# One PSUM pool and a reordered first stage in a linear-attention and gated-MLP block

## Chip, cores and metric

The kernel runs on one core of a Trainium2 chip. The metric is the device time of one execution in microseconds (us), of which some 2 us lie outside the span that the profile shows: 2.5 us in the profiled execution before. Medians are of several executions. A ratio is the mean time of one kernel's fast runs over that of the other's fast runs of the same rounds, so it is not quite the ratio of the medians that stand beside it.

Engines: PE is TensorE (matmuls), PEld its weight loads, DVE is VectorE, ACT is ScalarE, SP issues most of the DMAs. Timeline lines join neighbouring instructions of one kind; where a group reaches over the edge of the stretch that was asked for, only its part inside is counted.

## Reference

```python
# B=1, S=2048, D=1024, H=32 heads of 32, F=3584, all bf16
def A(x):                                   # linear attention
    q, k, v = split_heads(x @ wqkv)
    pq, pk = phi(q), phi(k)                 # where(t>0, t+1, exp(t)) + 1e-6
    kv = sum_s pk[s]^T v[s];  z = sum_s pk[s]
    return merge_heads((pq @ kv) / (pq @ z + 1e-6)) @ wo
def B(x):                                   # gated MLP
    return (relu(x @ W_gate) * (x @ W_up)) @ W_down
h  = x + A(layernorm(x))
h2 = h + B(layernorm(h))
```

## The kernel before

S is cut into 16 x tiles of 128 rows and 4 blocks of 512. The framework's scheduler puts each engine's instructions into one fixed order from their priorities and its own model; on the chip each engine then takes them in that order, each waiting for its semaphores. A tile drawn from a pool with `bufs=n` waits until the tile n draws earlier has been released.

```python
ps_a  = PSUM pool: tag "tp" 2 banks, tag "mm" 3 banks          # first stage
ps_kv = PSUM pool: kv_ps, 3 banks
for t in range(ST):                                            # 16 x tiles
    ... bn_stats, bn_aggr, Ln, Exp -> rstd;  xn = (x - mean) * rstd
    pt = ps_tp()
    for kc in range(KC):
        nc.tensor.transpose(pt[:, kc, :], xn[:, kc*P:(kc+1)*P], ident[:])
    nc.scalar.copy(out=xnT[:, :, t*P:(t+1)*P], in_=pt[:])      # 1.02 us
    for j in range(2 * NKB):                                   # 2 halves of K, 2 of V
        ps = ps_mm("kvp")
        for kc in range(KC):
            nc.tensor.matmul(ps, lhsT=xnT[:, kc, tile t], rhs=wkv_sb[:, kc, half j], ...)
        if j < NKB: phi_from_psum(ps, pk[half j])              # ACT exp, then two DVE operations
        else:       nc.scalar.copy(out=v_sb[half], in_=ps)
    for c in range(KC):
        nc.tensor.matmul(kv_ps[...], lhsT=pk[:, c], rhs=v_sb[:, c, :], ...)   # kv and z
    if t == 3: q_proj(0, ps_mm)
kvbd, zbd = kv_ps * mask;  q_proj(1, ps_mm)                    # pools ps_a, ps_kv end here

ps_b = PSUM pool: tags "tp", "pa", "pg", "pd", 2 banks each
attn_block(0)              # den, num, transposes, attn, LayerNorm, transposes of 4 tiles
q_proj(2), q_proj(3)       # on tag "pg": 2 banks; the scheduler mixes them into attn_block(0)
for b in range(4):
    attn_block(b + 1)      # mixed into the MLP by the scheduler
    mlp_block(b)           # gate on "pg", up on "pd", down on both
```

`q_proj(b)` makes pqT of block b: for each of 8 chunks, 8 matmuls into one bank, then phi into pqT. `attn_block(b)` starts with 32 tiny matmuls, `den<-zbd,pqT`.

## Time and profile before

| | before |
|---|---|
| time, median of 13 executions | 880.38 us (879.35 to 880.98) |
| span of the profiled execution | 878.0 us |
| matmuls | 5376 |

Summary of the profile page of the kernel before: the span, busy time by engine (share of the span, instructions), and the shares of the chain of work that ended last.

```profile
span 878.0 us, 12434 instructions
PE 854.8 (97%) x5376; PEld 488.7 (56%) x5376; DVE 288.9 (33%) x536; ACT 166.7 (19%) x305; POOL 3.6 (0%) x31
...
PE 94%; DVE 2%; ACT 2%; DMA 1%; issue 0%; SPq 0%; DVEq 0%
```

PE bounds the kernel.

The waits of PE in the kernel before: what PE waited for, us in total, number of times, longest.

```profile
PE tp L165 <- DVE xn L161: 9.0, 2, 6.0
PE kvp L173 <- ACT xnT L166: 4.6, 7, 0.7
PE qp L102 <- DVE pqT L88: 3.1, 3, 1.0
PE den L235 <- DVE pqT L88: 1.9, 1, 1.9
```

The head in the kernel before, from the timeline (start us, us, engine, line, operation, tiles, count, idle time before and what ended it): PE's first instructions, then two of ACT.

```profile
5.97 1.04 PE L165 MATMUL tp<-ident,xn 128*128 128x128 bf16 x8 [5.97 <-DVE xn L161]
10.06 0.93 PE L165 MATMUL tp<-ident,xn 128*128 128x128 bf16 x7 [3.06 <-DVE xn L161]
10.78 4.40 PE L173 MATMUL kvp<-wkv_sb,xnT 128*128 128x512 bf16 x11
...
9.22 0.20 ACT L159 ACTIVATE rstd<-lnv 128x1 f32<-128x1 f32 x1
9.33 0.99 ACT L166 COPY xnT<-tp 128x1024 bf16<-128x1024 bf16 x1
```

PE transposes tile 0 at 6 us, then stands for 3 us at the transposes of tile 1, which the order puts ahead of tile 0's first matmul. ACT copies tile 0 at 9.33 us only, behind tile 1's statistics.

The end of that stage in the kernel before (PE, then DVE), and one gap of the first attention block:

```profile
171.63 1.89 PE L102 MATMUL qp<-xnT,wq_sb 128*128 128x512 bf16 x8
175.40 0.96 PE L235 MATMUL den<-zbd,pqT 128*128 128x4 bf16 x32 [1.88 <-DVE pqT L88]
...
174.65 0.69 DVE L88 SCALAR_TENSOR_TENSOR pqT<-qp,phi_e 128x512 bf16<-128x512 f32 x1
...
187.76 0.59 PE L102 MATMUL qp<-xnT,wq_sb 128*128 128x512 bf16 x2 [1.03 <-DVE pqT L88]
```

### The profile page before, as it was taken

To read this page: it belongs to the slowest core of one execution; us is meant where nothing else is said; L and a number is where in the kernel's file an instruction comes from. 1 tells how busy PE (TensorE), PEld (TensorE's weight loads), DVE (VectorE), ACT (ScalarE), POOL (GpSimd) and SP (SyncE) were. 2 spreads that over 40 slices of the span, in tenths; PEclk is the share of its full clock that TensorE was granted. 3 is DMA by queue.
4 is the path that set the end of the run, shared out by engine and by line. 5 is a ranking of instruction groups with operands and counts; after the bars stand their busy time and mean duration, and the time that the engine had idled before them with its cause. 6 is when DMAs were issued, how large, how long until landed. Compare 5 with 4: busy or idle time off the path is not lost.

```text
span 878.0 us, 12434 instructions
## 1 busy us (share of the span) xinstructions
PE 854.8 (97%) x5376; PEld 488.7 (56%) x5376; DVE 288.9 (33%) x536; ACT 166.7 (19%) x305; POOL 3.6 (0%) x31
## 2 busy tenths in 40 slices
PE   5999999999999999999999999999999999999998
PEld 2444544444444445885444478744444885444687
DVE  4674332676762121116512110363212012212111
ACT  3443443322222111001211100022111001111100
POOL 0000000000000000000000000000000000000000
PEclk9999999999999999999999999999999999999999
DMA  9600000630024445651344555414353764353152
GB/s 322 228 25 25 1 1 1 216 96 25 13 76 153 149 140 184 189 167 61 120 154 135 191 175 174 133 49 133 130 190 111 217 180 136 127 192 97 42 174 73
DMA packets 133926, 109.85 MB, mean 125 GB/s; under 512 B 3824, under 2 KB 128752, under 8 KB 133872
## 3 DMA queue, kind: packets, MB, share of 16 engines
q1 hardware_dynamic: 133872, 109.07, 39.9%
q8 instruction: 42, 0.69, 0.3%
q14 instruction: 12, 0.10, 0.0%
HBM read 104.86 MB, written 4.19 MB: 124 GB/s over the span
## 4 chain that ended last, share of the span: by engine, by line
PE 94%; DVE 2%; ACT 2%; DMA 1%; issue 0%; SPq 0%; DVEq 0%
PE down L322 22%; PE gate L301 22%; PE up L305 21%; PE kvp L173 13%; PE attn L270 6%; PE qp L102 6%; PE tp L286 1%; PE kv_ps L184 1%; PE tp L260 1%; ACT xnT L166 1%; PE num L249 1%; DMA x_sb<-in_A_x_dram 1%; ACT v_sb L180 0%; DVE o_sb L253 0%; DVE h L272 0%; PE den L235 0%
## 5 line engine op out<-in xcount | busy, mean ns | idle before, releaser
L301 PE MATMUL gate<-hnT,wg_sb 128*128 128x512 bf16 x896 | 214.9, 379 | 0.0
L305 PE MATMUL up<-hnT,wu_sb 128*128 128x512 bf16 x896 | 214.6, 379 | 0.0
L322 PE MATMUL down<-wd_sb,hhT 128*128 128x256 bf16 x1792 | 196.3, 273 | 0.0
L322 PEld LDWEIGHTS <-hhT 128*128 128x128 bf16 x1792 | 175.3, 98 | 21.2
L309 DVE TENSOR_TENSOR hhT<-up,rg 128x512 bf16<-128x512 f32 x112 | 77.3, 690 | 269.4 <-PE up L305 266.6
L308 ACT ACTIVATE rg<-gate 128x512 bf16<-128x512 f32 x112 | 66.9, 597 | 474.2 <-PE gate L301 474.2
L305 PEld LDWEIGHTS <-wu_sb 128*128 128x128 bf16 x896 | 87.3, 98 | 102.4
L301 PEld LDWEIGHTS <-wg_sb 128*128 128x128 bf16 x896 | 86.8, 98 | 99.7
L173 PE MATMUL kvp<-wkv_sb,xnT 128*128 128x512 bf16 x512 | 116.4, 383 | 4.6 <-ACT xnT L166 4.6
L173 PEld LDWEIGHTS <-xnT 128*128 128x128 bf16 x512 | 49.3, 99 | 61.9 <-ACT xnT L166 5.8
L327 DVE TENSOR_TENSOR o_t<-down,h 128x256 bf16<-128x256 f32 x64 | 24.2, 419 | 171.4 <-PE down L322 169.5
L102 PE MATMUL qp<-xnT,wq_sb 128*128 128x512 bf16 x256 | 59.7, 379 | 3.1 <-DVE pqT L88 3.1
L270 PE MATMUL attn<-wo_sb,oT 128*128 128x512 bf16 x256 | 58.2, 380 | 0.0
L86 DVE TENSOR_SCALAR phi_e<-phi_e 128x512 f32<-128x512 f32 x64 | 26.9, 420 | 70.1 <-ACT phi_e L84 70.1
L270 PEld LDWEIGHTS <-oT 128*128 128x128 bf16 x256 | 23.8, 98 | 33.0 <-DVE oT L262 6.3
L102 PEld LDWEIGHTS <-wq_sb 128*128 128x128 bf16 x256 | 24.2, 98 | 29.0 <-issue 4.3
L272 DVE TENSOR_TENSOR h<-attn,x_res 128x512 bf16<-128x512 f32 x32 | 22.1, 691 | 32.8 <-PE attn L270 32.7
L84 ACT ACTIVATE phi_e<-qp 128x512 f32<-128x512 f32 x32 | 19.1, 597 | 50.4 <-PE qp L102 50.4
L84 ACT ACTIVATE phi_e<-kvp 128x512 f32<-128x512 f32 x32 | 19.1, 596 | 38.2 <-PE kvp L173 38.2
L180 ACT CAST v_sb<-kvp 128x512 bf16<-128x512 f32 x32 | 18.7, 585 | 32.9 <-PE kvp L173 32.9
L153 DVE BATCH_NORM_STATS2 stats<-x_sb 128x6 f32<-128x512 bf16 x32 | 20.6, 672 | 7.9 <-DMA x_sb<-in_A_x_dram 7.9
L88 DVE SCALAR_TENSOR_TENSOR pqT<-qp,phi_e 128x512 bf16<-128x512 f32 x32 | 22.1, 691 | 1.0
(41 smaller groups left out, 264.2 us busy)
## 6 DMA issues: line engine op xcount, KB each, us to landing
wg_sb<-in_B_W_gate_dram SPq DMA_DIRECT2D x28, 1024.0 KB, 5.2
wu_sb<-in_B_W_up_dram SPq DMA_DIRECT2D x28, 1024.0 KB, 7.4
wd_sb<-in_B_W_down_dram SPq DMA_DIRECT2D x112, 256.0 KB, 2.9
x_sb<-in_A_x_dram SPq DMA_DIRECT2D x16, 256.0 KB, 6.6
wkv_sb<-in_A_wqkv_dram SPq DMA_DIRECT2D x4, 1024.0 KB, 9.4
x_res<-in_A_x_dram SPq DMA_DIRECT2D x16, 256.0 KB, 2.6
out_dram<-o_t SPq DMA_DIRECT2D x32, 128.0 KB, 1.8
wq_sb<-in_A_wqkv_dram SPq DMA_DIRECT2D x2, 1024.0 KB, 11.2
```

Source lines behind the costliest of these rows:

```text
L84: nc.scalar.activation(out=e[:], in_=ps_ap, func=ACT.Exp)
L86: nc.vector.tensor_scalar(out=e2[:], in0=e[:], scalar1=1.0, scalar2=PHI_EPS, op0=ALU.min, op1=ALU.add)
L88: nc.vector.scalar_tensor_tensor(out=dst_ap, in0=ps_ap, scalar=0.0, in1=e2[:], op0=ALU.max, op1=ALU.add)
L102: nc.tensor.matmul(ps[:, :TB], lhsT=wq_sb[:, kc, c * P:(c + 1) * P], rhs=xnT[:, kc, b * TB:(b + 1) * TB], start=(kc == 0), stop=(kc == KC ...
L173: nc.tensor.matmul(ps[:, :NW], lhsT=xnT[:, kc, t * P:(t + 1) * P], rhs=wkv_sb[:, kc, j * NW:(j + 1) * NW], start=(kc == 0), stop=(kc == KC ...
L270: nc.tensor.matmul(ps[:, :NW], lhsT=oT[:, c, :], rhs=wo_sb[:, c, j * NW:(j + 1) * NW], start=(c == 0), stop=(c == KC - 1))
L301: nc.tensor.matmul(g_ps[:, :TB], lhsT=wg_sb[:, kc, fi * P:(fi + 1) * P], rhs=hnT[:, kc, :], start=(kc == 0), stop=(kc == KC - 1))
L305: nc.tensor.matmul(u_ps[:, :TB], lhsT=wu_sb[:, kc, fi * P:(fi + 1) * P], rhs=hnT[:, kc, :], start=(kc == 0), stop=(kc == KC - 1))
L308: nc.scalar.activation(out=rg[:], in_=g_ps[:, :TB], func=ACT.Relu)
L309: nc.vector.tensor_tensor(out=hhT[:, f, :], in0=u_ps[:, :TB], in1=rg[:], op=ALU.mult)
L322: nc.tensor.matmul(accs[tt // 2][:, tt % 2, :], lhsT=hhT[:, f, tt * P:(tt + 1) * P], rhs=wd_sb[:, fi, :], start=(f == 0 and tt % 2 == 0), ...
L327: nc.vector.tensor_tensor(out=o_ts[tt][:, q * QW:(q + 1) * QW], in0=accs[tt // 2][:, tt % 2, :], in1=h_tiles[t][:, q * QW:(q + 1) * QW], o ...
```

## The change

The intent is to keep PE from waiting in the first stage and at its borders:

- One PSUM pool for the whole kernel: tp 2 banks, x 2, y 4. kv_ps takes 3 of the y banks until the masks have read it. The late q_proj, gate, up and down share y.
- LayerNorm and transposes of tile t+1 come before K of tile t; K of four tiles comes before V of four tiles; the kv_ps matmuls come one tile late.
- The start is in a hand-made order on PE, ACT and DVE, and the first copy is split between DVE and ACT.
- Another DMA order at the start; half of the last stores are issued by ACT.

No matmul is added or removed. The core of the diff (cuts marked):

```diff
+    pspool = ctx.enter_context(tc.tile_pool(name="ps", bufs=1, space=PSUM))
+    def ps_x(nm="x"):  return pspool.tile([P, 512], FP32, tag="x", bufs=2, name=nm)
+    def ps_y(nm="y"):  return pspool.tile([P, 512], FP32, tag="y", bufs=4, name=nm)
+    def ps_xy(nm="xy"): ...                       # x, x, y in turn
-        ps_a = ...tile_pool(name="ps_a", ...)     # and ps_kv; ps_b after the first stage
-            return ps_a.tile([P, 512], FP32, tag="mm", bufs=3, name=nm)
+        ps_mm = ps_xy
+        kv_ps = [ps_y("kv_ps") for _ in range(n_kv_banks)]
...                                                # x0, wk0, x1, wk1, x2, x3, wv0, wv1, x4, ...
+            if t == 0 and KC >= 2:
+                nc.vector.tensor_copy(out=xnT[:, 0:KC // 2, tile t], in_=pt[:, 0:KC // 2, :])
+                nc.scalar.copy(out=xnT[:, KC // 2:KC, tile t], in_=pt[:, KC // 2:KC, :])
+            else:
+                nc.scalar.copy(out=xnT[:, :, t * P:(t + 1) * P], in_=pt[:])
...
+        with tc.manual_schedule(engines={ET.PE, ET.Activation, ET.DVE}):
+            ln_T(0)
+            xn1 = ln_x(1)
+            pk0 = kproj(0, [0])
+            tp_x(1, xn1)
+            kproj(0, [1], pk0)
+        for g in range(NTB):
+            for tt in range(TPB):                  # K of four tiles
+                ...
+                if t + 1 < ST: ln_T(t + 1)
+                pks[t] = kproj(t)
+                if tt == 0: kv_acc()
+            for tt in range(TPB):                  # V of four; kv_ps of the tile before
+                vproj_kv(t, pks.pop(t))
+            if g < NQA - 1: q_proj(g, ps_mm, kv_acc)
...
-                g_ps = ps_b.tile([P, 512], FP32, tag="pg", bufs=2, name="gate")
+                g_ps = ps_y("gate")
-        q_proj(b, lambda nm: ps_b.tile([P, 512], FP32, tag="pg", bufs=2, name=nm))
+        q_proj(b, ps_y)
...
+                    eng = nc.scalar if (last block, last quarter, tt % 2 == 1) else nc.sync
```

More of the change, by code (lines that the diff above doesn't have):

```diff
@@ L73, in block_kernel, with ps_tp, ps_x, ps_y @@
         nc.gpsimd.memset(mask[hh * Dh:(hh + 1) * Dh, P + hh:P + hh + 1], 1.0)
+    pspool = ctx.enter_context(tc.tile_pool(name="ps", bufs=1, space=PSUM))
+    _xy = [0]
+    def ps_tp():
+        return pspool.tile([P, KC, P], BF16, tag="tp", bufs=2, name="tp")
+    def ps_x(nm="x"):
+        return pspool.tile([P, 512], FP32, tag="x", bufs=2, name=nm)
+    def ps_y(nm="y"):
+        return pspool.tile([P, 512], FP32, tag="y", bufs=4, name=nm)
+    def ps_xy(nm="xy"):
+        _xy[0] += 1
+        return ps_x(nm) if _xy[0] % 3 != 0 else ps_y(nm)
     pq_pool = ctx.enter_context(tc.tile_pool(name="pq", bufs=1))
@@ L96, in block_kernel, with q_proj @@
     wqkv_v = wqkv.rearrange("(kc p) n -> p kc n", p=P)
-    def q_proj(b, ps_fn):
+    def q_proj(b, ps_fn, after_first=None):
         for c in range(KC):
@@ L105, in q_proj @@
             phi_from_psum(ps[:, :TB], pqT[:, c, b * TB:(b + 1) * TB], qwork, TB)
+            if c == 0 and after_first is not None:
+                after_first()
     NQA = min(2, NTB)
     with ExitStack() as actx:
-        ps_a = actx.enter_context(tc.tile_pool(name="ps_a", bufs=1, space=PSUM))
-        ps_kv = actx.enter_context(tc.tile_pool(name="ps_kv", bufs=1, space=PSUM))
         apool = actx.enter_context(tc.tile_pool(name="apool", bufs=1))
@@ L115, in block_kernel @@
         asmall = actx.enter_context(tc.tile_pool(name="asmall", bufs=4))
-        def ps_tp():
-            return ps_a.tile([P, KC, P], BF16, tag="tp", bufs=2, name="tp")
-        def ps_mm(nm="mm"):
-            return ps_a.tile([P, 512], FP32, tag="mm", bufs=3, name=nm)
+        ps_mm = ps_xy
         wkv_sb = apool.tile([P, KC, 2 * D], BF16, name="wkv_sb")
-        kv_ps = ps_kv.tile([P, n_kv_banks, 512], FP32, name="kv_ps")
+        kv_ps = [ps_y("kv_ps") for _ in range(n_kv_banks)]
         x_tiles = {}
@@ L133, in block_kernel @@
         load_x(0)
-        for j in range(2 * NKB):
+        nxt = 1
+        for j in range(NKB):
             nc.sync.dma_start(out=wkv_sb[:, :, j * NW:(j + 1) * NW],
                               in_=wqkv_v[:, :, D + j * NW:D + (j + 1) * NW])
-            if j == 0 and ST > 1:
-                load_x(1)
-        for t in range(2, min(4, ST)):
-            load_x(t)
+            if nxt < min(TPB, ST):
+                load_x(nxt)
+                nxt += 1
+        while nxt < min(TPB, ST):
+            load_x(nxt)
+            nxt += 1
+        for j in range(NKB, 2 * NKB):
+            nc.sync.dma_start(out=wkv_sb[:, :, j * NW:(j + 1) * NW],
+                              in_=wqkv_v[:, :, D + j * NW:D + (j + 1) * NW])
+        while nxt < min(6, ST):
+            load_x(nxt)
+            nxt += 1
         for j in range(NKB):
@@ L143, in block_kernel, with ln_x @@
         nc.sync.dma_start(out=wo_sb[:], in_=wo.rearrange("(kc p) n -> p kc n", p=P))
-        for t in range(ST):
+        def ln_x(t):
             if t not in x_tiles:
@@ L162, in block_kernel, with tp_x @@
                                     op0=ALU.subtract, op1=ALU.mult)
+            return xn
+        def tp_x(t, xn):
             pt = ps_tp()
@@ L165, in block_kernel, with ln_T, kproj @@
                 nc.tensor.transpose(pt[:, kc, :], xn[:, kc * P:(kc + 1) * P], ident[:])
-            nc.scalar.copy(out=xnT[:, :, t * P:(t + 1) * P], in_=pt[:])
-            pk = awork.tile([P, D], BF16, tag="pk", name="pk")
-            v_sb = awork.tile([P, KC, NDW], BF16, tag="v_sb", name="v_sb")
-            nc.gpsimd.memset(v_sb[:, :, P:NDW], 1.0)
-            for j in range(2 * NKB):
-                ps = ps_mm("kvp")
+            if t == 0 and KC >= 2:
+                nc.vector.tensor_copy(out=xnT[:, 0:KC // 2, t * P:(t + 1) * P], in_=pt[:, 0:KC // 2, :])
+                nc.scalar.copy(out=xnT[:, KC // 2:KC, t * P:(t + 1) * P], in_=pt[:, KC // 2:KC, :])
+            else:
+                nc.scalar.copy(out=xnT[:, :, t * P:(t + 1) * P], in_=pt[:])
+        def ln_T(t):
+            tp_x(t, ln_x(t))
+        def kproj(t, js=range(NKB), pk=None):
+            if pk is None:
+                pk = awork.tile([P, D], BF16, tag="pk", bufs=TPB + 2, name="pk")
+            for j in js:
+                ps = ps_mm("kp")
                 for kc in range(KC):
@@ L175, in block_kernel, with kv_acc @@
                                      start=(kc == 0), stop=(kc == KC - 1))
-                if j < NKB:
-                    phi_from_psum(ps[:, :NW], pk[:, j * NW:(j + 1) * NW], awork, NW)
-                else:
-                    jj = j - NKB
-                    nc.scalar.copy(out=v_sb[:, jj * CPB:(jj + 1) * CPB, 0:P],
-                                   in_=ps[:, :NW].rearrange("p (c e) -> p c e", e=P))
+                phi_from_psum(ps[:, :NW], pk[:, j * NW:(j + 1) * NW], awork, NW)
+            return pk
+        pend = []
+        def kv_acc():
+            if not pend:
+                return
+            t, pk, v_sb = pend.pop()
             for c in range(KC):
                 bnk, i = divmod(c, GPB)
-                nc.tensor.matmul(kv_ps[:, bnk, i * NDW:(i + 1) * NDW],
+                nc.tensor.matmul(kv_ps[bnk][:, i * NDW:(i + 1) * NDW],
                                  lhsT=pk[:, c * P:(c + 1) * P], rhs=v_sb[:, c, :],
@@ L187, in block_kernel @@
                                  skip_group_check=True)
-            if (t + 1) % TPB == 0 and t // TPB < NQA - 1:
-                q_proj(t // TPB, ps_mm)
-        for c in range(KC):
-            bnk, i = divmod(c, GPB)
-            nc.vector.tensor_tensor(out=kvbd[:, c, :], in0=kv_ps[:, bnk, i * NDW:i * NDW + P],
-                                    in1=mask[:, 0:P], op=ALU.mult)
-            nc.vector.tensor_tensor(out=zbd[:, c, :], in0=kv_ps[:, bnk, i * NDW + P:(i + 1) * NDW],
-                                    in1=mask[:, P:NDW], op=ALU.mult)
@@ L196, in block_kernel, with vproj_kv @@
-        q_proj(NQA - 1, ps_mm)
-    ps_b = ctx.enter_context(tc.tile_pool(name="ps_b", bufs=1, space=PSUM))
-    def ps_tp2():
-        return ps_b.tile([P, KC, P], BF16, tag="tp", bufs=2, name="tp")
-    def ps_pa(nm="pa"):
-        return ps_b.tile([P, 512], FP32, tag="pa", bufs=2, name=nm)
-    def ps_pg(nm="pg"):
-        return ps_b.tile([P, 2, HB], FP32, tag="pg", bufs=2, name=nm)
-    def ps_pd(nm="pd"):
-        return ps_b.tile([P, 2, QW], FP32, tag="pd", bufs=2, name=nm)
+        def vproj_kv(t, pk):
+            v_sb = awork.tile([P, KC, NDW], BF16, tag="v_sb", bufs=3, name="v_sb")
+            nc.gpsimd.memset(v_sb[:, :, P:NDW], 1.0)
+            for jj in range(NKB):
+                j = NKB + jj
+                ps = ps_mm("vp")
+                for kc in range(KC):
+                    nc.tensor.matmul(ps[:, :NW], lhsT=xnT[:, kc, t * P:(t + 1) * P],
+                                     rhs=wkv_sb[:, kc, j * NW:(j + 1) * NW],
+                                     start=(kc == 0), stop=(kc == KC - 1))
+                nc.scalar.copy(out=v_sb[:, jj * CPB:(jj + 1) * CPB, 0:P],
+                               in_=ps[:, :NW].rearrange("p (c e) -> p c e", e=P))
+            kv_acc()
+            pend.append((t, pk, v_sb))
@@ new lines, in block_kernel @@
+        ET = mybir.EngineType
+        with tc.manual_schedule(engines={ET.PE, ET.Activation, ET.DVE}):
[5 more added lines that the diff above has]
+        for g in range(NTB):
+            pks = {}
+            for tt in range(TPB):
+                t = g * TPB + tt
+                if t == 0:
+                    pks[0] = pk0
+                    continue
+                if t + 1 < ST:
+                    ln_T(t + 1)
+                pks[t] = kproj(t)
+                if tt == 0:
+                    kv_acc()
+            for tt in range(TPB):
+                t = g * TPB + tt
+                vproj_kv(t, pks.pop(t))
+            if g < NQA - 1:
+                q_proj(g, ps_mm, kv_acc)
@@ new lines, in last_kv @@
+        def last_kv():
+            kv_acc()
+            for c in range(KC):
+                bnk, i = divmod(c, GPB)
+                nc.vector.tensor_tensor(out=kvbd[:, c, :], in0=kv_ps[bnk][:, i * NDW:i * NDW + P],
+                                        in1=mask[:, 0:P], op=ALU.mult)
+                nc.vector.tensor_tensor(out=zbd[:, c, :], in0=kv_ps[bnk][:, i * NDW + P:(i + 1) * NDW],
+                                        in1=mask[:, P:NDW], op=ALU.mult)
+        q_proj(NQA - 1, ps_mm, last_kv)
@@ L212, in block_kernel, with ps_pair @@
+    ps_tp2 = ps_tp
+    ps_pa = ps_x
+    def ps_pair(nm="pair"):
+        return pspool.tile([P, 2, QW], FP32, tag="y", bufs=4, name=nm)
     bwork = ctx.enter_context(tc.tile_pool(name="bwork", bufs=2, side="right"))
@@ L302, in mlp_block @@
                                      start=(kc == 0), stop=(kc == KC - 1))
-                u_ps = ps_b.tile([P, 512], FP32, tag="pd", bufs=2, name="up")
+                u_ps = ps_y("up")
                 for kc in range(KC):
@@ L314, in mlp_block @@
         for q in range(NQ):
-            accs = [(ps_pg("down") if i % 2 == 0 else ps_pd("down")) for i in range(npair)]
+            accs = [ps_pair("down") for i in range(npair)]
             for g in range(NFG):
@@ L330, in mlp_block @@
                     q0 = q - (q % 2)
-                    nc.sync.dma_start(out=of[t * P:(t + 1) * P, q0 * QW:(q + 1) * QW],
-                                      in_=o_ts[tt][:, q0 * QW:(q + 1) * QW])
+                    eng = nc.scalar if (b == NTB - 1 and q == NQ - 1 and tt % 2 == 1) else nc.sync
+                    eng.dma_start(out=of[t * P:(t + 1) * P, q0 * QW:(q + 1) * QW],
+                                  in_=o_ts[tt][:, q0 * QW:(q + 1) * QW])
         for tt in range(TPB):
```

## The prediction

> **What bounds it now.** TensorE: the page has PE busy 854.8 of 878.0 us and PE 94% of the chain that ended last. Eight 128x512 matmuls take 1.73 us (216 ns each; timeline), 448 down matmuls 48.91 us (109 ns each); from 270 to 395 us PE has no idle. No matmul is added or removed, so only idle or slow PE time can be won. By timeline, chain and waits that is:
>
> - Head: the first K/V matmul starts at 10.78 us. PE's order puts 7 transposes of x tile 1 (landed 7.42, xn done 10.0) ahead of it, and the ACT copy of tile 0's transpose, ready at 7.0, stands behind tile 1's statistics (9.33).
> - The first 8 matmuls run 427 ns apart, until about 14.4 us. The Trainium skill (TensorE: Matmul & The Clock Gate, the HAM clock gate) says the array runs at half clock until about 3.4 us of activity; the trace agrees, although the clock view shows 1.00. About 1.7 us, which stays.
> - Attention-input stage, to 173.5 us: 16.85 us per two x tiles. At pure rate 64 matmuls of 216 ns and 32 small ones of 56 to 58 ns take 15.7: 1.1 us lost, nearly all PE waiting for ACT's 1.02 us xnT copy. About 7 pairs: 8 us.
> - Then 1.9 us before den and three waits of 1.03 us in the first attention block, all for DVE writing pqT (q_proj has two PSUM buffers there).
> - Tail: last matmuls near 874.3, four output DMAs issued in 1.82 us, end at 878.
>
> **What the change does.** One PSUM pool (tp 2, x 2, y 4 banks); K of four tiles, then V of four; transposes of tile t+1 before K of tile t; kv_ps one tile late; a hand-ordered start with the first copy split on DVE and ACT; another DMA order; half of the last stores issued by ACT. The built order agrees: tp x8, kp x8, tp x8, kp x12.
>
> **Estimate (from the durations above).**
> 1. Head: K can start near 7.7 us (7.0 plus half a copy). But DVE's order has a statistic of x tile 2 before xn of tile 1, and that tile lands near 11 us (2.9 MB at some 330 GB/s): PE idles about 1.5 us there, and about 1.5 us for xn of tiles 2 and 4, as DVE carries phi (1.12 us per half) and statistics. Net gain 0.5.
> 2. xnT copy hidden behind 16 K matmuls, kv matmuls without waits: 7.
> 3. q_proj with four buffers: of 3.1 us, 2.5, as DVE comes near 90% there. The den wait stays: 0.2.
> 4. Tail: the skill (Trainium Kernel Development and Optimization, Key Constraints) says that issuing from several queues saves only issue time: 0.2.
> 5. MLP: same four banks, no idle: 0.
>
> Sum about 10.5: **869.5 us** predicted, 865.5 to 873.5 for 8 in 10. Faster by over 2% (under 862.4): 0.04; within 2%: 0.955; slower: 0.005.
>
> **Right if**: first K matmul near 7.7 us; PE idles 1 to 2 us before tile 1's transposes, xn behind a DMA wait; PE's wait for xnT (4.6 us) is gone; stage A ends near 166 us; the 1.03 us waits shrink to near nothing; MLP blocks keep their 167.0 us period.
>
> **Wrong if**: x tile 2 lands elsewhere; K phases become DVE-bound (phi 2.24 plus LayerNorm 2.06 us per tile against 3.94 of PE) and PSUM runs out; DVE delays the attention chain; shared y banks stall the MLP.

## More of the kernel before

The Trainium skill (Perfetto Trace Analysis, Identifying the Most-Contended Engine) warns that matmul busy time is a poor measure of the distance to the roofline because matmuls are pipelined, and this trace agrees: a 128x512 matmul is recorded as 379 ns long, but back to back they start 216 ns apart. So I count from start to start. At the spacing each shape reaches when nothing holds it (216 ns for 512 columns, 109 for 256, 57.5 for 132, 55.8 for 128, 25.5 for the 4 columns of den) the 5376 matmuls take 842.8 us, not 854.8. The remaining 35.2 us of the span are what any change of order can work on.

The steady state of the first stage in the kernel before, PE in the timeline:

```profile
75.50 0.40 PE L184 MATMUL kv_ps<-v_sb,pk 128*128 128x132 bf16 x4
75.73 0.66 PE L165 MATMUL tp<-ident,xn 128*128 128x128 bf16 x9
77.05 7.08 PE L173 MATMUL kvp<-wkv_sb,xnT 128*128 128x512 bf16 x32 [0.66 <-ACT xnT L166]
83.97 0.40 PE L184 MATMUL kv_ps<-v_sb,pk 128*128 128x132 bf16 x4
84.20 0.59 PE L173 MATMUL kvp<-wkv_sb,xnT 128*128 128x512 bf16 x2
84.81 0.39 PE L184 MATMUL kv_ps<-v_sb,pk 128*128 128x132 bf16 x4
```

There are two losses here. Before the 32 kvp matmuls PE waits for ACT's copy of the transposes. And the second four kv_ps matmuls start at 84.81 us, although the two kvp matmuls ahead of them need only 0.43 us from 84.20: another 0.17 us, with no idle time shown, because the kvp matmul's record covers it. They wait for ACT's copy of the second half of v_sb (in an earlier tile that copy ends at 27.93 us and these matmuls start at 27.98).

## The result

| | before | after |
|---|---|---|
| time, median | 880.38 us (13 executions) | 864.30 us (8 executions, 864.16 to 864.71) |
| ratio | | 0.9819 (0.9809 to 0.9828) |
| span of the profiled execution | 878.0 us | 862.1 us |

The change wins 16.1 us, 1.8%. The prediction was 10.5 us (869.5 us, range 865.5 to 873.5): within 2%, as forecast, but 1.2 us below the range.

The summary of the profile page after:

```profile
span 862.1 us, 12429 instructions
PE 850.3 (99%) x5376; PEld 487.8 (57%) x5376; DVE 288.5 (33%) x537; ACT 167.1 (19%) x305; POOL 3.3 (0%) x31
...
PE 95%; DVE 2%; DMA 1%; ACT 1%; issue 0%; SPq 0%; DVEq 0%
```

PE's waits after:

```profile
PE tp L188 <- DVE xn L181: 7.0, 2, 6.2
PE kp L204 <- DVE xnT L190: 0.5, 1, 0.5
PE tp L353 <- DVE hn L349: 0.2, 1, 0.2
```

Three of the four waits are gone. 6.2 of the 7.0 us left are the start itself. The head after, PE in the timeline, then DVE:

```profile
6.23 1.04 PE L188 MATMUL tp<-ident,xn 128*128 128x128 bf16 x8 [6.23 <-DVE xn L181]
7.79 3.59 PE L204 MATMUL kp<-wkv_sb,xnT 128*128 128x512 bf16 x8 [0.52 <-DVE xnT L190]
12.15 0.62 PE L188 MATMUL tp<-ident,xn 128*128 128x128 bf16 x8 [0.78 <-DVE xn L181]
12.61 2.75 PE L204 MATMUL kp<-wkv_sb,xnT 128*128 128x512 bf16 x12
...
10.96 0.69 DVE L173 BATCH_NORM_STATS2 stats<-x_sb 128x6 f32<-128x512 bf16 x1 [1.79 <-DMA x_sb<-in_A_x_dram]
11.57 0.53 DVE L181 TENSOR_SCALAR xn<-x_sb,mv,rstd 128x1024 bf16<-128x1024 bf16 x1
```

As predicted, K starts at 7.8 us, and xn of tile 1 stands in DVE's order behind a statistic of tile 2, which lands at 10.96 us.

The steady state after: no gap anywhere in these lines, and the 8 kv_ps matmuls of a tile run in one piece.

```profile
87.31 3.62 PE L204 MATMUL kp<-wkv_sb,xnT 128*128 128x512 bf16 x16
90.76 0.63 PE L218 MATMUL kv_ps<-v_sb,pk 128*128 128x132 bf16 x8
91.23 0.61 PE L188 MATMUL tp<-ident,xn 128*128 128x128 bf16 x8
91.67 3.62 PE L204 MATMUL kp<-wkv_sb,xnT 128*128 128x512 bf16 x16
```

The end of the stage and the first attention block after (PE, then DVE, then PE again):

```profile
159.81 3.83 PE L118 MATMUL qp<-xnT,wq_sb 128*128 128x512 bf16 x17
163.57 0.94 PE L302 MATMUL den<-zbd,pqT 128*128 128x4 bf16 x32
...
164.76 0.68 DVE L104 SCALAR_TENSOR_TENSOR pqT<-qp,phi_e 128x512 bf16<-128x512 f32 x1
...
174.20 3.40 PE L118 MATMUL qp<-xnT,wq_sb 128*128 128x512 bf16 x15
177.44 0.61 PE L353 MATMUL tp<-ident,hn 128*128 128x128 bf16 x8
```

den starts at 163.57 us, before DVE has even begun the last phi of q_proj(1) (164.76 us). So den never needed that data: den of block 0 reads what q_proj(0) wrote long before. My prediction had taken it for a data wait.

The whole difference, counted from start to start in the two traces (each row is the time by which matmuls start later than the pure rate allows, put to the wait named there; first and last row are the time before the first and after the last matmul):

| us | before | after | won | predicted |
|---|---|---|---|---|
| until the first transpose | 5.97 | 6.23 | | |
| waits in the head (first copy, xn of tiles 1, 2, 4) | 3.31 | 2.46 | | |
| half-rate matmuls at the start | 2.47 | 1.76 | | |
| these three, the head | 11.75 | 10.45 | 1.3 | 0.5 |
| K/V matmuls waiting for ACT's xnT copy | 5.79 | 0 | 5.8 | |
| kv_ps waiting for ACT's second v_sb copy | 2.97 | 0 | 3.0 | |
| these two | 8.76 | 0 | 8.8 | 7 |
| q_proj in the first attention block | 3.60 | 0 | 3.6 | 2.5 |
| den | 2.04 | 0.09 | 1.95 | 0.2 |
| all other | 5.2 | 5.1 | 0.1 | 0 |
| after the last matmul | 3.85 | 3.66 | 0.2 | 0.2 |
| sum | 35.2 | 19.3 | 15.9 | 10.4 |

### The profile page after: what moved, and what is told of

Its sections match the earlier page's. It is cut to its first block, busy times and chain, and to the rows that moved or that the text cites. A ratio compares the mean times of both kernels' runs of the same rounds, so it can differ in the third digit from the quotient of the medians.

```text
span 862.1 us, 12429 instructions
## 1 busy us (share of the span) xinstructions
PE 850.3 (99%) x5376; PEld 487.8 (57%) x5376; DVE 288.5 (33%) x537; ACT 167.1 (19%) x305; POOL 3.3 (0%) x31
## 4 chain that ended last, share of the span: by engine, by line
PE 95%; DVE 2%; DMA 1%; ACT 1%; issue 0%; SPq 0%; DVEq 0%
PE down L389 23%; PE gate L368 22%; PE up L372 22%; PE attn L337 7%; PE vp L230 6%; PE qp L118 6%; PE kp L204 5%; PE tp L353 1%; DMA x_sb<-in_A_x_dram 1%; PE num L316 1%; PE kv_ps L218 1%; PE tp L327 1%; PE tp L188 1%; DVE stats L173 0%; PE den L302 0%; DVE hn L349 0%
## 5 line engine op out<-in xcount | busy, mean ns | idle before, releaser
L204 PE MATMUL kp<-wkv_sb,xnT 128*128 128x512 bf16 x256 | 59.6, 387 | 0.5 <-DVE xnT L190 0.5
L230 PE MATMUL vp<-wkv_sb,xnT 128*128 128x512 bf16 x256 | 57.2, 379 | 0.0
L233 ACT CAST v_sb<-vp 128x512 bf16<-128x512 f32 x32 | 18.7, 584 | 35.1 <-PE vp L230 35.1
```

The source lines that it names most:

```text
L204: nc.tensor.matmul(ps[:, :NW], lhsT=xnT[:, kc, t * P:(t + 1) * P], rhs=wkv_sb[:, kc, j * NW:(j + 1) * NW], start=(kc == 0), stop=(kc == KC ...
L230: nc.tensor.matmul(ps[:, :NW], lhsT=xnT[:, kc, t * P:(t + 1) * P], rhs=wkv_sb[:, kc, j * NW:(j + 1) * NW], start=(kc == 0), stop=(kc == KC ...
```

## Experiments

All twelve runs gave correct results. "The control" is the changed kernel itself, run again.

### One pool, the bank counts left alone (b_onepool)

Is the wait before den the handover from one set of PSUM pools to the next? This is the kernel before with its three pools made into one. Each use keeps as many banks as it had; only the borders between pools go.

```diff
-        ps_a  = ...tile_pool(name="ps_a", bufs=1, space=PSUM)
-        ps_kv = ...tile_pool(name="ps_kv", bufs=1, space=PSUM)
-            return ps_a.tile([P, 512], FP32, tag="mm", bufs=3, name=nm)
+            tag = "pa" if _n[0] % 3 != 0 else "pg"
+            return ps_b.tile([P, 512], FP32, tag=tag, bufs=2, name=nm)
-        kv_ps = ps_kv.tile([P, n_kv_banks, 512], FP32, name="kv_ps")
+        kv_ps = [ps_b.tile([P, 512], FP32, tag=tg, bufs=2, name="kv_ps") for tg in ("pg", "pd", "pd")]
```

> The kernel before, with one PSUM pool for the whole kernel in place of three (the bank counts stay: tp 2, matmul 3 and kv 3 in the first stage, q_proj 2 later). Theory A, that the 2.0 us before den were the handover from one set of pools to the next: that wait goes, about 878.4 us (minus 2.0), and the three waits of about 1 us in the first attention block stay. Rival, that den waits for data (the pqT of the last q_proj matmul): no change, 880.4 us, den still starts some 1.9 us after the last q_proj matmul.

Measured: 878.96 us against 880.66 for the kernel before beside it, ratio 0.9977 (0.9960 to 0.9994), which is 2.0 us. PE in the timeline of this run:

```profile
169.81 4.70 PE L102 MATMUL qp<-xnT,wq_sb 128*128 128x512 bf16 x21
174.43 0.94 PE L236 MATMUL den<-zbd,pqT 128*128 128x4 bf16 x32
```

den follows q_proj without a gap. From start to start its wait fell from 2.04 to 0.09 us; q_proj's waits stayed (3.25 us). Theory A holds and the data wait is refuted: the border between the pools was the wait. The DVE instruction that ended it in the kernel before, the last write of pqT, is also the last reader of the old pool's banks, which is how I explain that it was named.

### Four shared banks for q_proj (b_four, a_twobufs)

The one-pool kernel, with pg and pd made one tag of four banks (b_four); and from the other side, the changed kernel with its y tag split in two pairs (a_twobufs).

```diff
 b_four, against b_onepool
-        q_proj(b, lambda nm: ps_b.tile([P, 512], FP32, tag="pg", bufs=2, name=nm))
+        q_proj(b, lambda nm: ps_b.tile([P, 512], FP32, tag="y", bufs=4, name=nm))
   (gate, up, down, and kv_ps likewise)
 a_twobufs, against the changed kernel
-                g_ps = ps_y("gate")
+                g_ps = ps_y("gate", "y0")      # tags y0 and y1, 2 banks each
-        q_proj(b, ps_y)
+        q_proj(b, lambda nm: ps_y(nm, "y0"))
   (up and down likewise; kv_ps on y0, y1, y1)
```

> The one-pool kernel, with q_proj of the later blocks, gate, up and down sharing four banks in place of two and two. Theory: q_proj was held by two PSUM buffers; the waits of 1.2 us (3.6 in all) go and no later one comes, about 874.8 us. Rival, that DVE is too busy there (near 90%) to write pqT in time: the waits shrink by less than half, or turn up before the attention block's own matmuls, over 876.5 us.

> The changed kernel with its four y banks split in two pairs, so that the late q_proj, gate and up have two banks each, as before the change, in one pool still. Theory: the three or four waits of 1.2 us in the first attention block come back (3.6 us), the wait before den does not: about 867.9 us. Rival, that the banks were not what held q_proj, but the place that the scheduler gives it: 864.4 us.

Measured: b_four 875.11 us (ratio 0.9935, 0.9920 to 0.9950), 3.85 us less than b_onepool beside it; in its trace PE waits for pqT nowhere. a_twobufs 867.17 us (ratio 0.9847, 0.9832 to 0.9861), 2.9 us more than the changed kernel had in its own rounds; the wait before den stayed away, and q_proj's is back among PE's waits:

```profile
PE qp L122 <- DVE pqT L108: 2.4, 3, 1.0
```

So two banks held q_proj, and DVE was not too busy. The Trainium skill (Perfetto Trace Analysis, Optimization Strategy) says that the same gap repeating on the engine that should be saturated can mean too few buffers in SBUF or PSUM; here the three gaps of 1.19 us from start to start in the kernel before were just that (in a_twobufs 0.54, 1.19 and 1.19; its trace lacks 69 matmul records, none of them at these gaps). With two banks the scheduler also places fewer q_proj matmuls between the attention block's steps (9 to 12 at a time, not 15), so the two runs need not agree to the tenth.

### Transposes ahead (b_ahead), and kv_ps one tile late (b_kvlate)

Each is the kernel before with one part of the change.

```diff
 b_ahead
-        for t in range(ST):
+        def ln_T(t):
             ... LayerNorm, transposes, copy of tile t
+        ln_T(0)
+        for t in range(ST):
+            if t + 1 < ST:
+                ln_T(t + 1)
 b_kvlate
-            for c in range(KC):
-                ... kv_ps matmuls of tile t
+            kv_acc()                       # those of the tile before
+            pend.append((t, pk, v_sb))     # pk and v_sb get a third buffer
```

> The kernel before, with LayerNorm and transposes of x tile t+1 issued before the K and V matmuls of tile t, and nothing else. Theory: PE's wait for ACT's xnT copy (0.82 us each, 5.8 us in all before) goes and the wait of kv_ps for the v_sb copy (3.0 us in all) stays: about 874.6 us. The rival of my prediction, that nearly all of the loss of this stage was the xnT copy (8 us): about 872.4 us.

> The kernel before, with the kv_ps matmuls of tile t issued after the V matmuls of tile t+1, and nothing else. Theory: the 3.0 us that kv_ps waited for the second half of v_sb go. The built order now also has 8 kv_ps and 8 further transposes between a tile's transposes and its first K matmul, about 0.9 us of work that would hide most of the 1.02 us copy too: about 873 us if both go, 877.4 us if only the kv_ps waits go, 880.4 us if neither mattered.

Measured beside each other: b_ahead 875.78 us (0.9944, 0.9930 to 0.9959), b_kvlate 874.59 us (0.9931, 0.9916 to 0.9946). In b_ahead's trace the copy wait is gone and kv_ps still waits, 3.2 us; in b_kvlate's kv_ps waits nowhere and the copy wait fell from 5.8 to 2.5 us. So my prediction's "1.1 us lost per pair, nearly all PE waiting for the copy" was two losses, and they overlap: work put between a tile's transposes and its first K matmul hides the copy, whichever work it is.

b_ahead came out about 1 us above the theory. Its first slow phase happened to last 12 matmuls (8 in the kernel before), and two of its four executions show a mean clock of 0.998 and took 876.2 and 876.4 us, against 875.3 and 875.4 for the other two. b_kvlate's profiled execution is such a one, and shows what happened. Stretches of time of that run: us, busy us (instructions) of PE, PEld, DVE, ACT and POOL, then the granted clock, DMA share and GB/s; below them PE in the timeline.

```profile
166.00:169.00 3.00, 1.13 (x8) 0.38 (x7) 2.22 (x4) 0.60 (x1) 0.00 (x0) 1.00 1.15 315
171.00:174.40 3.40, 3.40 (x14) 1.44 (x13) 1.92 (x4) 0.60 (x1) 0.00 (x0) 0.50 1.02 264
...
168.92 0.96 PE L245 MATMUL den<-zbd,pqT 128*128 128x4 bf16 x32 [1.87 <-DVE pqT L88]
170.49 2.73 PE L102 MATMUL qp<-xnT,wq_sb 128*128 128x512 bf16 x7
```

After the wait before den and its tiny matmuls the clock fell to 0.50 for 3.4 us, and the seven qp matmuls took 2.73 us instead of 1.67. The two executions with clock 0.998 took 875.2 and 875.0 us, the two with 1.000 took 874.1 and 874.2. So the wait before den cost its 2.0 us, and in some executions 1 us more. The record fits this: of the executions whose clock was listed, 9 of 31 show 0.998 in the three kernels with this wait (before, b_ahead, b_kvlate) and none of 50 in the others.

That bears on the ratios. In the rounds of b_sum, a_twobufs, a_best and a_best2, four of the seven executions of the kernel before had the clock of 0.998, and its mean was 881.06 us (880.64 in the rounds of the four head runs below). So those four ratios are about 0.05% too good beside the others.

### The four parts together (b_sum)

The kernel before with b_ahead, b_kvlate and b_four's edits joined; its head, DMA order, tail, and K and V of one tile together are left.

> The kernel before with four parts of the change alone: transposes of tile t+1 ahead, kv_ps one tile late, one PSUM pool, four shared banks. Its head, its DMA order, its tail and K and V of one tile together stay as before. Theory: these four are worth 5.8 + 3.0 + 2.0 + 3.6 = 14.4 us, so about 866.1 us, and what is left to the changed kernel (864.4) is its head (1.3) and tail (0.3). Rival, that grouping K of four tiles ahead of V of four is worth something of its own: over 867.5 us.

Measured: 866.19 us, ratio 0.9833 (0.9816 to 0.9849), against 866.1 expected. Within that interval, putting K and V into groups of four is worth nothing of its own: the 1.9 us between this and the changed kernel (2.3 us by the medians of the spans) are near the 1.5 us that the table gives to head and tail, and the slow phase in the head of b_sum's profiled execution lasted 12 K matmuls, not 8, which is 0.8 us. The tail's 0.2 us was not tested by itself. (This trace lacks 68 matmul records, none of them in the slow phase, so only that phase and the time are used.)

### The head (a_ctrl, a_nomanual, a_x2first, a_warm)

Four runs on one chip with five rounds: the control, and three edits of the changed kernel.

```diff
 a_nomanual
-        with tc.manual_schedule(engines={ET.PE, ET.Activation, ET.DVE}):
-            ln_T(0); xn1 = ln_x(1); pk0 = kproj(0, [0]); tp_x(1, xn1); kproj(0, [1], pk0)
+        ln_T(0); xn1 = ln_x(1); pk0 = kproj(0, [0]); tp_x(1, xn1); kproj(0, [1], pk0)
 a_x2first
-            if nxt < min(TPB, ST):
+            while j == 0 and nxt < min(3, ST):     # x0, wk0, x1, x2, wk1, x3, ...
 a_warm, first in the hand-ordered start
+            wsrc = apool.tile([P, 512], BF16, name="wsrc")
+            nc.vector.memset(wsrc[:], 0.0)
+            wps = ps_x("warm")
+            for _ in range(12):
+                nc.tensor.matmul(wps[:], lhsT=wsrc[:, 0:P], rhs=wsrc[:], start=True, stop=True)
```

> The changed kernel again, unaltered, as the control for the three runs beside it: 864.3 us, ratio to the kernel before 0.982.

> The changed kernel without the hand-ordered start; the rest of the change stays. The built order puts xn of x tile 1 ahead of DVE's half of the first copy and 4 of its transposes ahead of the first K matmul, so K starts near 10.4 us in place of 7.8, as in the kernel before; in return the 1.2 us wait before tile 1's transposes goes. If the hand-ordered start is what the head gains, plus 1.2 us, about 865.5 us. If the clock's slow phase or the DMA order decide instead, no change, 864.3 us.

> The changed kernel with x tile 2 loaded before the second K weight piece. Theory: PE's 1.2 us before the transposes of tile 1 is DVE standing at a statistic of tile 2, whose load lands at 10.9 us; landing near 8.4 us it frees xn by 11.1 us, while the slow-clock K matmuls still run: minus 1.0 us, about 863.3 us. Rival, that the weights bound the head: K's second half then waits for its later piece (0.8 us later), and nothing is gained, 864.3 us.

> The changed kernel with 12 matmuls of zeros on TensorE before the first transposes, from about 1 us to 6 us, into a bank that nothing reads. Theory: the first 8 K matmuls take 427 ns only because PE had just woken; busy before, they take 216 ns, minus 1.7 us, and the first 8 transposes 56 ns, minus 0.3; the built order also has xn of tile 1 ahead of tile 2's statistic, so of the 1.2 us wait there some 0.7 stays. Together about 862.0 us. Rival, that the first matmuls are slow for another reason (weights landing, or the copy halves): still 427 ns apart and no gain, 864.3 us.

| run | median us (range) | ratio to before (interval) |
|---|---|---|
| a_ctrl | 864.52 (864.13 to 867.61) | 0.9828 (0.9813 to 0.9843) |
| a_nomanual | 865.83 (865.03 to 866.10) | 0.9830 (0.9816 to 0.9843) |
| a_x2first | 863.43 (863.20 to 865.32) | 0.9809 (0.9795 to 0.9822) |
| a_warm | 863.51 (863.00 to 864.13) | 0.9805 (0.9792 to 0.9818) |

The control scatters: two of its five executions took 866.0 and 867.6 us, and no trace of them exists to say why. So differences of 1 us here lean on the medians, and the intervals overlap.

Without the hand-made order K starts at 10.37 us (7.79 in the changed kernel, 10.78 in the kernel before): as in the kernel before, PE stands 3.0 us before the first transposes of tile 1, four of which the order puts ahead of K. In return PE no longer stops between the two halves of K (1.19 us in the changed kernel). The net loss is 1.3 us by the medians, as expected.

With x tile 2 first the three executions without a profile took 863.2 to 863.5 us, as expected, but the profiled one took 865.3: its K waited 1.49 us for its first weights, which landed at 8.5 us, and tile 1's transposes started at 12.3 us as before. The mechanism that I expected is not shown by the one trace there is; this stays open.

The zero matmuls settle the slow phase. PE in the timeline of a_warm:

```profile
1.18 4.22 PE L244 MATMUL warm<-wsrc 128*128 128x512 bf16 x12 [1.18 <-DVE wsrc L241]
6.16 0.62 PE L188 MATMUL tp<-ident,xn 128*128 128x128 bf16 x8 [0.76 <-DVE xn L181]
7.30 1.90 PE L204 MATMUL kp<-wkv_sb,xnT 128*128 128x512 bf16 x8 [0.52 <-DVE xnT L190]
9.92 0.62 PE L188 MATMUL tp<-ident,xn 128*128 128x128 bf16 x8 [0.72 <-DVE xn L181]
...
15.27 0.62 PE L188 MATMUL tp<-ident,xn 128*128 128x128 bf16 x8 [1.06 <-DVE xn L181]
```

The first 8 K matmuls take 1.90 us in place of 3.59, so neither weights nor copies had slowed them before: the slow phase is PE's own. But the median fell by 1.0 us only (0.65 us by the spans), not by the sum of 2.5 us that I expected: PE now arrives earlier and waits, 0.89 us from start to start before tile 1's transposes and 1.22 before tile 2's (0.19 in the changed kernel). The slow matmuls had hidden part of DVE's LayerNorm chain.

### A version that beats both (a_best, a_best2)

a_best joins a_warm and a_x2first. a_best2 joins a_warm with a longer hand-made start:

```diff
 a_best2, besides the zero matmuls
             tp_x(1, xn1)
+            xn2 = ln_x(2)
             kproj(0, [1], pk0)
+            pk1 = kproj(1, [0])
+            tp_x(2, xn2)
+            kproj(1, [1], pk1)
```

> The changed kernel with both the zero matmuls ahead of the first transposes and x tile 2 ahead of the second K weight piece. If their gains added, about 862.5 us. But with K at full rate PE is at the second K half by about 9.6 us, ahead of its piece of weights (now near 11) and of xn of tile 1: I expect no gain over the zero matmuls alone, 863.5 us.

> The changed kernel with the zero matmuls and a longer hand-ordered start: K of tile 1 begins ahead of tile 2's transposes, and DVE does the first phi and xn of tile 2 ahead of the rest. With the zero matmuls alone PE waits 1.2 us before tile 2's transposes; that should go: about 862.4 us. If DVE's load as such bounds the head, the wait only moves to tile 3 or 4: 863.5 us.

Measured: a_best 863.56 us (0.9805, 0.9790 to 0.9819), no gain over the zero matmuls alone, as expected. a_best2 862.85 us (862.82 to 862.92; 0.9796, 0.9782 to 0.9811). The wait before tile 2's transposes fell from 1.22 to 0.30 us; part of it moved to about 22 us, where a K matmul now starts 0.74 us late, behind DVE's phi (which frees its PSUM bank), and tile 4's transposes 0.58 us late. a_best2 is the fastest kernel, some 1.4 us under the changed kernel by the medians of their own rounds, though the two intervals of the ratio still touch. By the spans the gain is 1.1 us (861.0 against 862.1): 1.8 us lie outside the span there and 2.2 in the changed kernel, and no run says why. (The trace of a_best2 lacks 68 of 5388 matmul records.)

## Why the prediction was wrong

Its reading of the bound was right: PE at its own rate, no matmul removed, so only waits could go, and the MLP gave nothing (from one block's down matmuls to the next 167.04 us in both traces; "all other" moved by 0.1 us). K started at 7.79 us (predicted near 7.7), tile 2 landed at 10.96 (near 11), the xnT wait was gone, the 1.03 us waits were gone, and the tail gave 0.2 us. The first stage ended at 163.6 us, not near 166. The sum was 5.5 us short, in four terms:

1. **"The den wait stays: 0.2."** This step was false. 1.95 us were won. I took the releaser that the profile names, DVE writing pqT, for data that den needs; b_onepool shows that it was the border between two PSUM pools. The source would have told: den of block 0 reads what q_proj(0) wrote.
2. **"xnT copy hidden ..., kv matmuls without waits: 7."** The mechanism was right, the size was not: 8.8 us. The loss of the stage is 5.8 us for the copy and 3.0 us for kv_ps waiting for v_sb, 16 times. I had put "nearly all" to the copy because no idle time is shown before kv_ps, and rounded 8 down to 7. b_kvlate and b_ahead show the two losses apart.
3. **"Of 3.1 us, 2.5, as DVE comes near 90% there."** 3.6 us were won: the three waits are 1.19 us each from start to start, and DVE did not hold anything up (b_four).
4. **"Net gain 0.5" in the head.** 1.3 us: K starts 3.0 us earlier, less the waits. I had expected 3.0 us of waits for xn; there were 1.7, as the slow K matmuls, all eight, covered part of tile 1's wait, and DVE was ahead of the estimate for tiles 2 and 4.

All four errors have one sign: except for the copy's split, I discounted each gain for a conflict that I expected (DVE's load, a data dependence) without a number for the conflict.

## What to carry to other kernels

On an engine that bounds the kernel, sum its work at the start-to-start spacing of each shape and put every excess to a cause; idle times from recorded ends hide part of each wait and all of the short ones. Where a stage border shows a wait, ask whether the instruction needs the named data or only the buffer: here opening the next PSUM pool cost 2 us, and one pool for the whole kernel removed it. Before discounting a gain for a busy engine, check that a buffer count is not the cause, and remember that a gain in one step (PE at full rate in the head) can come back as a wait for the next.

## What the Trainium skill lacked or had wrong

- TensorE: Matmul & The Clock Gate (HAM oscillation; HAM is the activity monitor that gates PE's clock) gives as its rule that PE must not idle for more than about 3.4 us, or it falls back to half clock. In b_kvlate 1.87 us of idle followed by 32 matmuls of 4 columns in about 0.8 us was enough: clock 0.50 for 3.4 us in the profiled execution, and two of its four executions show the mean clock of 0.998 that goes with it. The same page tells of another kernel in which frequent short idles did this too, but gives no length for them. Whether thin matmuls count as busy, no run here tests.
- The same page (the HAM clock gate) says that the array starts at half clock and is released after about 3.4 us of activity. Here unbroken matmuls of zeros ran at half rate for 3.0 us in a_warm and for all 12, 5.1 us, in a_best. The granted clock reads 1.00 during such a first phase (10.8 to 14.2 us in the kernel before), while it does show 0.50 for the later one. The page warns that the trace's clock events are unreliable; it does not say that the first phase can be missing.
- Perfetto Trace Analysis says that matmul busy time misleads, and that a matmul's recorded end is an estimate. It does not say that the idle time before a matmul misleads for that reason: 16 waits of kv_ps, 3.0 us in all, have no line among PE's waits, and q_proj's three waits read 1.03 us for 1.19.
- No page names the border between two PSUM pools as a cost: 2.0 us here, with the wait put down to an instruction whose data were not needed.
